# The 24-point stages of batches 2 to 7 fire at the steps of the logits groups, and the first transform of a batch fires during the inverse of the batch before

## The chip, the cores and the metric

The kernel runs on one core of a Trainium2 chip. The metric is the device time of one execution in microseconds (us), taken as the median of several runs. Less is better.

## What is computed

For 8 batches of 3072 x 256 the reference filters in the frequency domain, then runs two token-wise layers. Cut to what matters:

```python
X = np.fft.rfft(x, axis=1)
y = np.fft.irfft(X * (filt_r + 1j * filt_i)[None], n=3072, axis=1)
x = y.reshape(8 * 3072, 256)
h = np.maximum(x @ w_in, 0.0)              # 256 -> 2048
x = h * h @ w_out                          # 2048 -> 256
logits = x @ phi                           # 32 slots
d = softmax(logits, axis=0)                # over all 24576 tokens
slot_out = experts(d.T @ x)                # 8 small experts
out = softmax(logits, axis=1) @ slot_out
```

## The kernel before, in words

The program is written out instruction by instruction, and every engine works through its own list in that order. There are three long phases: a prologue (weights, the whole transform of batch 0), a main loop, and an end with the experts and the output.

**The main loop** runs `pair(P)` for 384 values of P. One pair is 256 of the 2048 hidden features for one chunk of 512 tokens; 8 pairs make a chunk, 48 pairs a batch. A pair has four steps k = 0 to 3, and program time t = 2P + 0.5k counts them, so a batch is 96 units of t. Each step runs `layer` (three matmuls, L380 to L382, in fp32r on the whole array) on PSUM tile p0 in steps 0 and 1 and on p1 in steps 2 and 3. After p0 is full, ScalarE takes relu (L388) and VectorE multiplies (L389, which reads p0 as well, so p0 is free only after it). After p1 is full, ScalarE takes relu (L391) and GpSimd squares (L392). VectorE also transposes both results into hT (L399). In every odd pair, at k = 1, a logits group (`logit`, L408: 4 matmuls, which the profile counts as 8) stands behind the layer.

**The side work** is put into that loop by four streams (`dsp`, `late`, `fft`, `w`). Each entry has a due time; `run_streams` fires entries in order once their time has come, early ones without PSUM tiles ahead of the step's layer, all others behind it. Five PSUM banks are shared by all side work. An entry that needs more banks than are free at that place of the program holds the streams back until a later step.

- `fft` computes the next batch's filtering. `mm_a` (L141 to L143) is the 128-point transform, 12 times a batch: `split_x` (ScalarE L129, GpSimd L130) makes its input, `evac_a` (L151) and `store_a` write it to memory as S. `mm_b` (L187) is the 24-point transform, 8 times a batch, in 16 matmuls (32 in the profile) on 2 banks; `filt` (VectorE L198, two halves of two multiplies each) and `join` (GpSimd L207) apply the filter; `mm_g` (L220) is the inverse 24-point transform on 4 banks, which `evac_g` (ScalarE L229) empties and `store_g` writes to memory as G. Before, batches 2 to 7 have mm_a from t = 5 in steps of 1.5, mm_b at 30 + 6.6 i, and mm_g 4.5 later, all counted from the start of the batch ahead.
- `late` loads G and does the 128-point inverse: `mm_ai` (L320, two halves), `evac_ai` (L330) and `prep` (L343 on ScalarE, L346 on GpSimd), 6 times a batch.
- `dsp` is the softmax over tokens, once a chunk: `gather` (L447) at t = 4 from the chunk's start, `emax` (L452 to L455), `slot_in` (L499, 64 matmuls, 128 in the profile, on 4 banks) at 6.5, directly behind a logits group, and `accum` (VectorE L515) at 8 to 9.5.

The lines that set the order:

```python
    put(T, mm_b, i)                      # T = B0 + i * dB
    put(T + 0.5, filt, i, 0)
    put(T + 1.5, filt, i, 1)
    put(T + n["g"], mm_g, i)
    ...
    if k == 1 and P % 2 and P > 2:
        logit(P - 3)
    run_streams(t)
```

Of the kernel before, what the change touches and what calls it, by code (L numbers as in the profile page):

```python
# [38 lines left out]
def body(tc, x, cA, cAf, fwd, inv, flt, cst, w_in, w_out, phi, w1, w2, out):  # L39
# [10 lines left out]
    G = {}  # L50
# [22 lines left out]
    def put0(t, fn, *a):  # L73
        ev0[round(t, 3)].append((fn, a))
# [23 lines left out]
    def side():  # L98
        if G["nsd"]:
            return G["ps"].tile([128, 512], F32, tag="sd", name="sd", bufs=G["nsd"])  # L100
        k = free.pop(0)
        p = G["ps"].tile([128, 512], F32, tag=f"s{k}", name="sd")
        taken[id(p)] = k, p
        return p

    def done(p):

        if id(p) in taken:
            free.append(taken.pop(id(p))[0])


    def fft_events(b, pl, put, A0, dA, B0, dB, n, st):
        xv = x[b].rearrange("(p n) d -> p n d", n=N2)

        def big():
# [135 lines left out]
        if b == 0:  # L251
# [12 lines left out]
            for i in range(8):  # L264
                T = ST["B0"] + ST["dB"] * i
                put((.7, .75, 15)[i] if i < 3 else T - 6.5, load_c, i)
                put((.8, 9, 15.5)[i] if i < 3 else T - 6.4, load_f, i)
                put(18 + .1 * i if i < 3 else T - 6, load_s, i)
                put(T, mm_b, i)
                for r in range(2):  # L270
                    put(T + 1 + .5 * r, filt, i, r)
                    put(T + 1 + .5 * r, join, i, r)
# [8 lines left out]
        for u in range(12):  # L281
            T = A0 + u * dA
# [2 lines left out]
            put(T + 0.5, evac_a, u)  # L285
            put(T + 2.5, store_a, u)
        for i in range(8):
            T = B0 + i * dB
            put(T - 5.5, load_c, i)
            put(T - 5.5, load_f, i)  # L290
            put(T - 5, load_s, i)
            put(T, mm_b, i)
            put(T + 0.5, filt, i, 0)
            put(T + 1.5, filt, i, 1)
            put(T + 1, join, i, 0)
            put(T + 2, join, i, 1)
            put(T + n["g"], mm_g, i)
            for c in range(4):
                put(T + n["g"] + 0.5 + 0.5 * (c // 2), evac_g, i, c)
            put(T + n["lag"], store_g, i)  # L300

    def out_events(b, st, late):

        def load_g(g):
            t = G["mlp"].tile([128, 4, D], F32, tag="gin", name="gin")
            sync.dma_start(out=t, in_=st["G"][:, 4 * g:4 * g + 4, :])
            st["gi", g] = t

        def warm():

            p = side()
            for _ in range(7):
                pe.matmul(p[:, 0:416], cI, cst_t[:, 0:416], start=True, stop=True)
            done(p)

        def mm_ai(g, k):
            t = st["gi", g]
            p = side()
            for a in range(4):
                pe.matmul(  # L320
                    p[:, 128 * a:128 * a + 128], t[:, a, 128 * k:128 * k + 128], cI,
                    start=True, stop=True,
                )
            st["ai", g, k] = p

        def evac_ai(g, k):
            if k == 0:
                st["xt", g] = G["dsp"].tile([128, 2, CH], F32, tag="xt", name="xt")
            p = st.pop(("ai", g, k))
            act.activation(  # L330
                out=st["xt", g][:, k, :].rearrange("p (q a t) -> p a q t", q=4, a=4),
                in_=p.rearrange("p (a q t) -> p a q t", a=4, q=4), func=ACTF.Copy,
            )
            done(p)

        def prep(g, k):
            xt = st["xt", g]
            if k == 0:
                xo[b * NCB + g] = G["mlp"].tile([128, 2, 2, CH], F32R, tag="xo", name="xo", bufs=2)
            o = xo[b * NCB + g]  # L340
            h = k // 2
            if k % 2 == 0:
                act.activation(out=o[:, 0, h, :], in_=xt[:, h, :], func=ACTF.Copy)  # L343
            else:
                eng = vec if b + g == 0 and h else gps
                eng.tensor_tensor(  # L346
                    out=o[:, 1, h, :], in0=xt[:, h, :], in1=o.bitcast(F32)[:, 0, h, :], op=ALU.subtract
                )

        for g in range(NCB):  # L350
            T = 96 * b + 16 * g - 6
            put = late
            if T < 0:
                def put(t, fn, *a):
                    put0(ST["G0"] + ST["Gd"] * (t + 9), fn, *a)
            put(T - 3, load_g, g)
            if T < 0:
                put(T - 1, warm)
            put(T, mm_ai, g, 0)
            put(T + 0.5, mm_ai, g, 1)  # L360
            put(T + 0.5, evac_ai, g, 0)
            put(T + 1, evac_ai, g, 1)
            for k in range(4):
                put(T + 1.5 + 0.5 * k, prep, g, k)

    xo = {}

# [316 lines left out]
    def stream(nm, o=0):  # L684
        def put(t, fn, *a):
            streams[nm].append((t + o, fn, a))
        return put

    def fire(lst):
        for fn, a in lst:  # L690
            fn(*a)
# [19 lines left out]
    def open_main():  # L711
        first_c.__exit__(None, None, None)
        ps0_c.__exit__(None, None, None)
        G["ps_c"], G["ps"] = pool("ps", 1, PS)
        G["nsd"] = 0
        G["mlp_c"], G["mlp"] = pool("mlp", side="right")
        G["dsp_c"], G["dsp"] = pool("dsp", side="right")
# [36 lines left out]
    with tc.manual_schedule():  # L754
        put, late = stream("fft"), stream("late")
        st = {}
        put0(38, load_const)
        fft_events(0, lambda: first, put0, 0, 0, 0, 0, dict(f=17, u=12, c=4), st)
        out_events(0, st, late)
        def wput(t, *a):  # L760

# [15 lines left out]
        for t in sorted(ev0):  # L777
            if t >= ST["G0"] and not opened:
                opened = True
                open_main()  # L780
            fire(ev0[t])
        for b in range(1, NB):
            st = {}
            fft_events(
                b, lambda: G["fft"], stream("fft", 96 * (b - 1)), *((24, 1.1, 44.2, 4.6) if b == 1 else (5, 1.5, 30, 6.6)), dict(f=6, u=8, c=2, lag=7 if b == 1 else 9.5, g=3.5 if b == 1 else 4.5), st
            )
            out_events(b, st, late)
        for c in range(NCH - 1):
            dispatch_events(c, stream("dsp"))
# [200 lines left out]
        for g in range(NG):  # L990
            b, o = divmod(g, N2 // 4)
# [161 lines left out]
```

## Time and profile before

| | |
|---|---|
| median of 3 runs | 2124.04 us (2123.72 to 2124.53) |
| the profiled execution | 2123.9 us; its span, first to last instruction, 2122.1 us |
| PE (TensorE matmul) busy | 2044.6 us, 96% |
| VectorE (DVE) busy | 1376.1 us, 65% |
| ScalarE (ACT) busy | 887.0 us, 42% |
| GpSimd (POOL) busy | 850.2 us, 40% |
| mean granted TensorE clock | 0.984 of full speed |

A busy PE here is one that has a matmul in flight; starts of matmuls are measured, ends are modelled. So the rows below are read by starts: two neighbouring layer matmuls start 0.23 us apart when nothing hinders them, and what stands between a layer's last start and the next layer's first ones beyond that is the price of what lies between.

### The profile page before, as it was taken

To read this page: it belongs to the slowest core of one execution; us is meant where nothing else is said; L and a number is where in the kernel's file an instruction comes from. 1 tells how busy PE (TensorE), PEld (TensorE's weight loads), DVE (VectorE), ACT (ScalarE), POOL (GpSimd) and SP (SyncE) were. 2 spreads that over 40 slices of the span, in tenths; PEclk is the share of its full clock that TensorE was granted. 3 is DMA by queue.
4 is the path that set the end of the run, shared out by engine and by line. 5 is a ranking of instruction groups with operands and counts; after the bars stand their busy time and mean duration, and the time that the engine had idled before them with its cause. 6 is when DMAs were issued, how large, how long until landed. Compare 5 with 4: busy or idle time off the path is not lost.

```text
span 2122.1 us, 44747 instructions
## 1 busy us (share of the span) xinstructions
PE 2044.6 (96%) x18334; PEld 1287.0 (61%) x18334; DVE 1376.1 (65%) x2516; ACT 887.0 (42%) x1780; POOL 850.2 (40%) x881
## 2 busy tenths in 40 slices
PE   6799999999999999999999999999999999999987
PEld 3366556665666566665566556665566656666556
DVE  3685766566656666576666766667666766666648
ACT  2345434533354344534354334543444334333335
POOL 2425443444353343444344434444345443232324
PEclk7699999999999999999999999999999999999999
DMA  9744342344134332333233332334223433100579
GB/s 286 201 142 135 102 107 74 112 105 120 31 112 116 79 98 65 117 95 110 55 105 105 90 99 67 123 95 110 54 88 102 110 98 94 66 23 12 144 261 384
DMA packets 145037, 238.23 MB, mean 112 GB/s; under 512 B 14785, under 2 KB 97089, under 8 KB 144833
## 3 DMA queue, kind: packets, MB, share of 16 engines
q1 hardware_dynamic: 144688, 235.25, 36.8%
q8 instruction: 144, 2.36, 0.5%
q14 instruction: 61, 0.49, 0.1%
q0 software_dynamic: 144, 0.13, 0.0%
HBM read 154.59 MB, written 80.74 MB: 111 GB/s over the span
## 4 chain that ended last, share of the span: by engine, by line
PE 88%; DVE 6%; DMA 2%; issue 2%; ACT 1%; SPq 0%; POOL 0%; DVEq 0%; ACTq 0%; POOLq 0%
PE p L380 19%; PE p L381 16%; PE p L382 16%; PE sd L499 10%; PE L L408 9%; PE sd L320 4%; PE sd L220 3%; PE sd L187 3%; PE sd L447 2%; DVE u L198 2%; PE sd L141 1%; PE sd L142 1%; PE sd L143 1%; DVE h L389 1%; DVE hT L399 1%
## 5 line engine op out<-in xcount | busy, mean ns | idle before, releaser
L392 POOL TENSOR_TENSOR h<-h 128x512 f32<-128x512 f32 x384 | 399.7, 1041 | 959.6 <-ACT h L391 847.6
L380 PE MATMUL p<-xo,wiH 128*128 128x512 f32 x1536 | 668.7, 435 | 3.9 <-ACT xo L343 1.2
L381 PE MATMUL p<-xo,wiH 128*128 128x512 f32 x1536 | 608.1, 396 | 0.9 <-POOL xo L346 0.9
L382 PE MATMUL p<-xo,wiL 128*128 128x512 f32 x1536 | 607.3, 395 | 0.0
L389 DVE SCALAR_TENSOR_TENSOR h<-p,h 128x512 f32<-128x512 f32 x384 | 264.8, 690 | 448.4 <-ACT h L388 447.3
L399 DVE STREAM_TRANSPOSE hT<-h 128x512 f32<-128x512 f32 x768 | 515.8, 696 | 14.6 <-POOL h L392 3.6
L391 ACT ACTIVATE h<-p 128x512 f32<-128x512 f32 x384 | 229.9, 599 | 540.9 <-PE p L382 539.5
L380 PEld LDWEIGHTS p<-xo,wiH 128*128 128x128 f32 x1536 | 288.8, 188 | 255.6 <-issue 79.3
L388 ACT ACTIVATE h<-p 128x512 f32<-128x512 f32 x384 | 229.6, 598 | 284.3 <-PE p L382 280.9
L382 PEld LDWEIGHTS p<-xo,wiL 128*128 128x128 f32 x1536 | 289.3, 188 | 69.7
L381 PEld LDWEIGHTS p<-xo,wiH 128*128 128x128 f32 x1536 | 290.0, 189 | 58.8 <-issue 9.8
L499 PE MATMUL sd<-hT,eT 32*32 32x512 f32 x6144 | 224.5, 602 | 4.7 <-DVE eT L478 2.9
L207 POOL TENSOR_TENSOR u<-u 128x256 f32<-128x256 f32 x256 | 183.6, 742 | 111.9 <-DVE u L198 111.0
L408 PE MATMUL L<-h,wf 128*32 128x512 f32 x1536 | 205.6, 605 | 0.8 <-POOL h L392 0.8
L198 DVE TENSOR_TENSOR u<-sd,f 128x512 f32<-128x512 f32 x256 | 162.1, 677 | 54.6 <-PE sd L187 54.2
L499 PEld LDWEIGHTS sd<-hT,eT 32*32 32x32 f32 x6144 | 107.5, 103 | 118.3 <-issue 56.5
L515 DVE SCALAR_TENSOR_TENSOR ac<-ac,sc,sd 128x512 f32<-128x512 f32 x188 | 133.8, 733 | 55.0 <-PE sd L499 55.0
L130 POOL TENSOR_TENSOR u<-f,u 128x512 fp32r<-128x512 f32 x84 | 108.0, 1287 | 73.0 <-ACT u L129 72.5
L346 POOL TENSOR_TENSOR xo<-xt,xo 128x512 fp32r<-128x512 f32 x95 | 121.6, 1295 | 6.1 <-ACT xo L343 6.1
L320 PEld LDWEIGHTS sd<-cst_t,gin 128*128 128x128 f32 x768 | 96.6, 191 | 44.4 <-issue 21.8
L229 ACT ACTIVATE f<-sd 128x256 f32<-128x256 f32 x256 | 81.1, 387 | 91.7 <-PE sd L220 91.7
L330 ACT ACTIVATE xt<-sd 128x512 f32<-128x512 f32 x96 | 57.4, 598 | 123.6 <-PE sd L320 123.6
(107 smaller groups left out, 1580.5 us busy)
## 6 DMA issues: line engine op xcount, KB each, us to landing
f<-flt SPq DMA_DIRECT2D x64, 512.0 KB, 4.7
f<-x SPq DMA_DIRECT2D x48, 512.0 KB, 4.2
S<-u SPq DMA_DIRECT2D x96, 256.0 KB, 2.1
f<-S SPq DMA_DIRECT2D x128, 192.0 KB, 5.3
G<-f SPq DMA_DIRECT2D x128, 192.0 KB, 5.2
gin<-G SPq DMA_DIRECT2D x48, 512.0 KB, 6.2
out<-w1t SPq DMA_DIRECT2D x47, 512.0 KB, 5.1
wx<-w SPq DMA_DIRECT2D x34, 256.0 KB, 5.3
```

What stands on the lines that cost most here:

```text
L198: vec.tensor_tensor(out=u, in0=p.rearrange("p (h d) -> p h d", d=D), in1=f[:, 2 * r + k:2 * r + k + 1, :].to_broadcast([128, 2, D]), op=AL ...
L207: gps.tensor_tensor(out=a[:, h, :], in0=a[:, h, :], in1=b[:, 1 - h, :], op=ALU.add if h else ALU.subtract)
L380: pe.matmul(p, wh, x[:, 0, kk, :], start=(kk == 0), stop=False)
L381: pe.matmul(p, wh, x[:, 1, kk, :], start=False, stop=False)
L382: pe.matmul(p, wl, x[:, 0, kk, :], start=False, stop=(kk == 1))
L388: act.activation(out=h, in_=p, func=ACTF.Relu, scale=2.0 ** -16)
L389: vec.scalar_tensor_tensor(out=h, in0=p, scalar=0.0, in1=h, op0=ALU.max, op1=ALU.mult)
L391: act.activation(out=h, in_=p, func=ACTF.Relu, scale=2.0 ** -8)
L392: gps.tensor_tensor(out=h, in0=h, in1=h, op=ALU.mult)
L399: vec.transpose(hT[c][:, 2 * i + k, :], h2[P, k])
L408: pe.matmul(lg[c][32 * n:32 * n + 32, :], wf[:, f, :], h2.pop((P + n // 2, n % 2)), start=(f < 4), stop=(f >= FT - 4), tile_position=(0, 3 ...
L499: pe.matmul(S[r][32 * t:32 * t + 32, :], e[rows, o:o + 32], h[rows, :, o:o + 32], start=(a == 0), stop=(a == 3), tile_position=(32 * r, 32 ...
```

## The change

The functions that compute anything are the same. Three things move.

- For batches 2 to 7, mm_b and mm_g get lists of due times. The list is 4k + 2.5 without every fourth entry, that is, the steps of the logits groups without those that slot_in follows; even entries go to mm_b, odd ones to mm_g. mm_g then follows its mm_b by 4 or 8 units, and store_g follows mm_g by 3.5 (before 5).
- For batches 2 to 7 the first mm_a is due at -22 (before 5), that is, in the last quarter of the batch ahead.
- In the 128-point inverse, of all batches, the second mm_ai moves from T + 0.5 to T + 1, and its evac_ai and all prep by 0.5.

Batch 1 keeps its due times.

```diff
--- before.py
+++ after.py
@@ -109,7 +109,7 @@
             free.append(taken.pop(id(p))[0])
 
 
-    def fft_events(b, pl, put, A0, dA, B0, dB, n, st):
+    def fft_events(b, pl, put, A0, dA, TB, TG, n, st):
         xv = x[b].rearrange("(p n) d -> p n d", n=N2)
 
         def big():
@@ -285,7 +285,7 @@
             put(T + 0.5, evac_a, u)
             put(T + 2.5, store_a, u)
         for i in range(8):
-            T = B0 + i * dB
+            T = TB[i]
             put(T - 5.5, load_c, i)
             put(T - 5.5, load_f, i)
             put(T - 5, load_s, i)
@@ -294,10 +294,11 @@
             put(T + 1.5, filt, i, 1)
             put(T + 1, join, i, 0)
             put(T + 2, join, i, 1)
-            put(T + n["g"], mm_g, i)
+            T = TG[i]
+            put(T, mm_g, i)
             for c in range(4):
-                put(T + n["g"] + 0.5 + 0.5 * (c // 2), evac_g, i, c)
-            put(T + n["lag"], store_g, i)
+                put(T + 0.5 + 0.5 * (c // 2), evac_g, i, c)
+            put(T + 3.5, store_g, i)
 
     def out_events(b, st, late):
 
@@ -357,11 +358,11 @@
             if T < 0:
                 put(T - 1, warm)
             put(T, mm_ai, g, 0)
-            put(T + 0.5, mm_ai, g, 1)
             put(T + 0.5, evac_ai, g, 0)
-            put(T + 1, evac_ai, g, 1)
+            put(T + 1, mm_ai, g, 1)
+            put(T + 1.5, evac_ai, g, 1)
             for k in range(4):
-                put(T + 1.5 + 0.5 * k, prep, g, k)
+                put(T + 2 + 0.5 * k, prep, g, k)
 
     xo = {}
 
@@ -779,11 +780,15 @@
                 opened = True
                 open_main()
             fire(ev0[t])
+
+        grid = [4 * k + 2.5 for k in range(24) if k % 4 != 1]
         for b in range(1, NB):
             st = {}
-            fft_events(
-                b, lambda: G["fft"], stream("fft", 96 * (b - 1)), *((24, 1.1, 44.2, 4.6) if b == 1 else (5, 1.5, 30, 6.6)), dict(f=6, u=8, c=2, lag=7 if b == 1 else 9.5, g=3.5 if b == 1 else 4.5), st
-            )
+            if b == 1:
+                when = (24, 1.1, [44.2 + 4.6 * i for i in range(8)], [47.7 + 4.6 * i for i in range(8)])
+            else:
+                when = (-22, 1.5, grid[0:16:2], grid[1:16:2])
+            fft_events(b, lambda: G["fft"], stream("fft", 96 * (b - 1)), *when, dict(f=6, u=8, c=2), st)
             out_events(b, st, late)
         for c in range(NCH - 1):
             dispatch_events(c, stream("dsp"))
```

**What TensorE issues, at the sixth mm_b of batch 4.** Before, mm_g and mm_b stand together in an even pair (P = 172), with no logits:

```order
L382 MATMUL p<-xo,wiL 128x512
L220 MATMUL sd<-u,iv 64x256 x16
L187 MATMUL sd<-f_10191,fw 32x256 x16
L380 MATMUL p<-xo,wiH 128x512
L381 MATMUL p<-xo,wiH 128x512
L382 MATMUL p<-xo,wiL 128x512
L380 MATMUL p<-xo,wiH 128x512
L381 MATMUL p<-xo,wiH 128x512
L382 MATMUL p<-xo,wiL 128x512
L320 MATMUL sd<-cst_t,gin 128x128 x4
```

Now the same mm_b stands behind the logits of the odd pair that follows (lines below the edit are numbered one higher, so the layer is L381 to L383, logits L409, mm_ai L321):

```order
L321 MATMUL sd<-cst_t,gin 128x128 x4
L381 MATMUL p<-xo,wiH 128x512
L382 MATMUL p<-xo,wiH 128x512
L383 MATMUL p<-xo,wiL 128x512
L409 MATMUL L<-h,wf 32x512 x4
L187 MATMUL sd<-f_10328,fw 32x256 x16
L381 MATMUL p<-xo,wiH 128x512
L382 MATMUL p<-xo,wiH 128x512
L383 MATMUL p<-xo,wiL 128x512
```

The two groups have left the even pair, and mm_g no longer stands in front of mm_b. Over the whole program 42 more mm_g (all 48 of batches 2 to 7 now) and 43 mm_b stand directly behind logits; five further mm_b have one mm_a between. The number of even pairs with no side group between their last p0 matmul and the next pair's first rises from 111 to 154.

**What VectorE issues around a filter.** Before, at the sixth mm_b of batch 4, one transpose stands between the two halves of the filter (L198), and the L389 of the next pair behind them:

```order
L399 STREAM_TRANSPOSE hT<-h 128x512
L198 TENSOR_TENSOR u<-sd,f_10424 128x512 x2
L399 STREAM_TRANSPOSE hT<-h 128x512
L198 TENSOR_TENSOR u<-sd,f_10424 128x512 x2
L389 SCALAR_TENSOR_TENSOR h<-p,h 128x512
L399 STREAM_TRANSPOSE hT<-h 128x512 x2
```

Now, at the seventh mm_b of the same batch, which is one of those at 2.5 units in a chunk (L389 is now L390, L399 is L400, emax L453 to L456):

```order
L390 SCALAR_TENSOR_TENSOR h<-p,h 128x512
L198 TENSOR_TENSOR u<-sd,f_10565 128x512 x2
L400 STREAM_TRANSPOSE hT<-h 128x512 x2
L198 TENSOR_TENSOR u<-sd,f_10565 128x512 x2
L453 TENSOR_REDUCE mn<-sd 128x1
L455 TENSOR_TENSOR mn<-mn 128x1
L456 TENSOR_SCALAR nm<-mn 128x1
L390 SCALAR_TENSOR_TENSOR h<-p,h 128x512
```

Two transposes now stand between the halves, and for the three of eight mm_b that fall at 2.5 the three steps of emax stand between the filter and the L390 that frees p0.

## Rows read from the trace of the kernel before

**Rows 1.** Chain that ended last, by engine (page, part 4).

```profile
PE 88%; DVE 6%; DMA 2%; issue 2%; ACT 1%; SPq 0%; POOL 0%; DVEq 0%; ACTq 0%; POOLq 0%
```

**Rows 2.** Timeline of PE (start us, us, line, operation, out<-in): logits alone.

```profile
1002.81 0.39 PE L382 MATMUL p<-xo,wiL 128*128 128x512 f32 x1
...
1004.46 0.40 PE L381 MATMUL p<-xo,wiH 128*128 128x512 f32 x1
```

**Rows 3.** Timeline of PE: inverse group L220 alone.

```profile
1005.40 0.39 PE L382 MATMUL p<-xo,wiL 128*128 128x512 f32 x1
...
1007.10 0.40 PE L381 MATMUL p<-xo,wiH 128*128 128x512 f32 x1
```

**Rows 4.** Timeline of PE: 24-point group L187 alone.

```profile
1011.28 0.40 PE L382 MATMUL p<-xo,wiL 128*128 128x512 f32 x1
...
1012.97 0.39 PE L381 MATMUL p<-xo,wiH 128*128 128x512 f32 x1
```

**Rows 5.** Timeline of PE: L220 directly behind logits.

```profile
917.90 0.39 PE L382 MATMUL p<-xo,wiL 128*128 128x512 f32 x1
918.22 1.06 PE L408 MATMUL L<-h,wf 128*32 128x512 f32 x8
919.22 1.12 PE L220 MATMUL sd<-u,iv 32*64 32x256 f32 x32
...
920.60 0.40 PE L381 MATMUL p<-xo,wiH 128*128 128x512 f32 x1
```

**Rows 6.** Timeline of PE: L220 and L187 in one step.

```profile
977.93 0.40 PE L382 MATMUL p<-xo,wiL 128*128 128x512 f32 x1
...
979.69 1.10 PE L220 MATMUL sd<-u,iv 32*64 32x256 f32 x26 [0.78 <-DVE ac L515]
981.28 1.37 PE L187 MATMUL sd<-f,fw 48*32 48x256 f32 x32 [0.48 <-ACT f L229]
...
982.92 0.40 PE L381 MATMUL p<-xo,wiH 128*128 128x512 f32 x1
```

**Rows 7.** Timeline of PE: L220 with a wait; slot_in without and with one.

```profile
938.25 1.85 PE L220 MATMUL sd<-u,iv 32*64 32x256 f32 x32
...
970.17 4.47 PE L499 MATMUL sd<-hT,eT 32*32 32x512 f32 x128
...
1014.52 1.05 PE L499 MATMUL sd<-hT,eT 32*32 32x512 f32 x6
1015.87 4.40 PE L499 MATMUL sd<-hT,eT 32*32 32x512 f32 x122 [0.29 <-DVE u L198]
```

**Rows 8.** Timeline of PE: from an even pair to an odd one.

```profile
1010.07 0.39 PE L381 MATMUL p<-xo,wiH 128*128 128x512 f32 x1
1010.30 0.40 PE L382 MATMUL p<-xo,wiL 128*128 128x512 f32 x1
1010.71 0.51 PE L380 MATMUL p<-xo,wiH 128*128 128x512 f32 x1
```

**Rows 9.** Waits, PE: who waited for whom: us in total, times, longest.

```profile
PEld p L380 <- DVE h L389: 52.0, 117, 0.6
```

**Rows 10.** Timeline of DVE, then PE: a filter ahead of L389.

```profile
997.80 1.29 DVE L198 TENSOR_TENSOR u<-sd,f 128x512 f32<-128x512 f32 x2 [0.90 <-PE sd L187]
999.01 0.70 DVE L399 STREAM_TRANSPOSE hT<-h 128x512 f32<-128x512 f32 x1
...
1000.80 0.68 DVE L389 SCALAR_TENSOR_TENSOR h<-p,h 128x512 f32<-128x512 f32 x1
...
1001.54 0.50 PE L380 MATMUL p<-xo,wiH 128*128 128x512 f32 x1
```

**Rows 11.** Timeline of DVE: emax.

```profile
1008.63 0.69 DVE L452 TENSOR_REDUCE mn<-sd 128x1 f32<-128x512 f32 x1 [2.73 <-PE sd L447]
...
1009.55 0.15 DVE L455 TENSOR_SCALAR nm<-mn 128x1 f32<-128x1 f32 x1
```

**Rows 12.** Lines, PE: busy us, mean ns of one, idle before.

```profile
L447 PE MATMUL sd<-lp,cst_t 128*128 128x512 f32 x96 | 49.1, 592 | 0.7 <-ACT lp L442 0.7
```

## The prediction

> **What bounds the kernel now.** I read the chain of waits first, then TensorE's timeline. The chain runs through PE for 88% of the span [rows 1], and PE's list is in order, so almost every gap between PE's starts is time. The gaps are of three kinds, and I price each from starts. Two neighbouring layer matmuls start 0.23 apart [rows 8]; from a layer's last start ahead of a side group to the second layer start behind it would be 0.47 without the group, and the rest is the group's price.
>
> First, the edges of a group. Logits alone cost 1004.46 - 1002.81 - 0.47 = 1.18 [rows 2], an inverse group (mm_g) alone 1.23 [rows 3], a 24-point group (mm_b) alone 1.22 [rows 4]. An inverse group directly behind logits makes 920.60 - 917.90 - 0.47 = 2.23 for both [rows 5]: 0.18 less than the 1.18 + 1.23 apart.
>
> Second, waits for PSUM banks. Where mm_g and mm_b come in one step the pair costs 982.92 - 977.93 - 0.47 = 4.52, with mm_g waiting for accum (L515) and mm_b for mm_g's evacuation (L229) [rows 6]; unhindered they would cost 1.23 + 1.22 = 2.45. A second mm_g takes 1.85 [rows 7] for 1.12 [rows 5]. And slot_in takes 4.47 on most occasions, but from 1014.52 to 1020.27 = 5.75 where mm_b's banks are still held by the filter (L198) [rows 7]. In the timeline each of the three returns once in each of batches 2 to 7.
>
> Third, the step from an even pair to an odd one. p0 is free only when L388 and L389 are through, and if no side group lies between, the next pair's L380 starts 0.41 instead of 0.23 behind the last L382 [rows 8], and its first two steps take 0.57 instead of 0.47 [rows 8, 4]: 0.28 in all. The waits view has PE's weight loads held by L389 117 times [rows 9]. From an odd pair to an even one the logits group gives the slack, so this stall does not occur there.
>
> **The change part by part.** No instruction on TensorE is added or removed; the sum is all about who stands beside whom.
>
> *Edges.* 42 more mm_g stand directly behind logits: 42 x 0.18 = 7.6 saved. For 43 mm_b the trace of before has no case behind logits. The bounds are 0 and the 0.18 of mm_g; I take 0.18, since logits end in the same way for either follower and mm_b alone costs what mm_g alone costs [rows 3, 4]: 7.7. Five mm_b have an mm_a between and save nothing. Together -15.3.
>
> *The bank waits.* mm_g now never falls on accum's steps (8 to 9.5 in a chunk; its places are 2.5, 10.5 and 14.5), it never stands ahead of mm_b in the same step, and no mm_b falls within three units ahead of slot_in. So all three waits should go: 6 x (2.07 + 0.73 + 1.28) = -24.5. At 10.5 mm_g takes four banks of which accum had three or four; it stands behind a whole layer pair and logits, and accum's last read is due a unit earlier, so I add nothing.
>
> *The uncovered step.* mm_b and mm_g used to lie in even pairs about as often as not, and there covered the stall of 0.28. In odd pairs, behind logits, they cover nothing. The order gives 111 uncovered steps before and 154 now: 43 x 0.28 = +12.0.
>
> *The filter ahead of L389.* On VectorE both halves of the filter now stand ahead of the next L389. At such a place before, the chain from 997.80 to 1001.54 made PE wait 0.30, not 0.18 [rows 10]. Now there is one more transpose in it (from 999.01 to 1000.80 are a transpose and a filter half, and a half is 1.21, so 0.58), while PE has half a layer pair more to run, 0.70. So 30 of the 48 are as before or better: 0 (at worst 0.12 each, 3.6). For the 18 at 2.5 emax comes on top: 1008.63 to 1009.70 = 1.07 [rows 11], while PE gets a gather of 49.1 / 48 = 1.02 busy [rows 12], of which its starts feel a little less. Bounds 0 and 0.30 each; I take 0.2: +3.6.
>
> *What I cost at nothing.* The second mm_ai leaves its place behind logits; it uses the whole array like the layer (128*128), so it has no edge to share. If it had, 39 x 0.18 = 7.0 would be lost: kept for the range. The moved transform takes its whole train along: x loads, S stores, splits on ScalarE and GpSimd, and evacuations. On SP's queue each load keeps its lead of 5 units (a unit is some 2.5 us) over its user, and load_g still follows the last store_g by about a unit. On GpSimd the splits now stand beside one filter's joins and on ScalarE beside two inverse groups' evacuations; both engines are under half busy. What covers it is the lead of 2 units that a split has. Without that cover one stretch a batch could cost as much as the waits that go, 4.1.
>
> Sum: 2123.9 (the profiled execution, 0.14 under the median) - 15.3 - 24.5 + 12.0 + 3.6 = 2099.7, say **2100 us**, 1.1% less.
>
> **The rivals.**
>
> *Every change of form drains.* Logits work in 128*32 tiles and mm_b in 48*32 [rows 5, 4]. If the array had to empty between them as it does between layer and mm_b, the 7.7 would not come, and the time is 2107. For it: no row shows this neighbourship. Against it: mm_g's form differs from logits' as well and it saved 0.18. The Trainium skill (TensorEngine Tiling (Array Packing), Key Properties) says that changing the tiling mode, not merely the tile, drains TensorE. By that rule logits followed by mm_b is three changes instead of four, and by it alone the saving would be one drain. No run here yet shows which. Chance 0.10.
>
> *The waits come back in other places.* Five banks serve everything; mm_g takes four, and behind it mm_ai, mm_a or the gather want the fifth and then the ones that ScalarE has just emptied. In the last quarter of each batch mm_a now mixes with both. If half of the 24.5 stays in this form the time is 2112; if all of it, 2124, no change. For it: before, exactly such mixing made the waits. Against it: the new places are 4 units apart or more, and the evacuations are due 0.5 and 1 behind the group. Chance 0.09, of which 0.04 up to no change. That the groups would not follow logits at all is ruled out: the order shows that they do.
>
> *VectorE falls behind and every filter is paid by PE.* VectorE is 65% busy on average, but in a pair of pairs with a filter it has two filter halves, two L389, four transposes and at 2.5 also emax to do, and all in order ahead of the L389 that frees p0. If it enters such a stretch late, as it does when a transpose waits for GpSimd's square behind two joins, PE waits for a whole filter half: 48 x 1.21 = 58, and the time is 2158, **slower**. It turns from gain to loss at 24 / 48 = 0.5 per filter. The Trainium skill (TensorE: Matmul & The Clock Gate, the table at its head) calls VectorE's and GpSimd's queues strictly first in, first out; nothing can pass the filter. The trace agrees so far: L389 starts 3.00 behind the first half, at 1000.80 [rows 10]. Against it: that same place cost PE 0.12 more than usual, not 1.2. Chance 0.04.
>
> **How the numbers follow.** My forecast (waits gone, both kinds of group merged, stall added) has 0.77, and by its own bounds lies from 2093 (no emax term, some mm_a cover more) to 2107 (mm_ai loses its edge). The range goes on to the second rival's half and a little more: **2090 to 2116**. About 0.2% is what a measurement of this kernel can tell from no change, that is 4 us. Faster: 0.77 + 0.10 + 0.05 = 0.92; the same 0.04; slower 0.04.
>
> **What would show it.** In the profile after: L187 starts 1.00 behind logits' start and logits plus L187 cost about 2.23 (if 2.40, the first rival). No L220 waits for L515, and slot_in is about 4.47 everywhere in batches 2 to 7. The weight loads of L380's successor wait for L389 some 150 to 160 times instead of 117, still about 0.28 a piece; behind a mm_b at 2.5 a little more. If these waits grow to over 0.8 a piece the third rival is true. I am wrong if new rows appear in which L320, L141 or L447 wait for L229, or in which L389 waits for L198.

## The result

The changed kernel takes 2100.29 us (median of 5 runs, 2097.76 to 2102.23); the kernel before took 2124.53 in the runs beside it. The ratio is 0.9878, 95% interval 0.9863 to 0.9893: 24 us less, where 24 had been forecast. The range (2090 to 2116) holds it.

### The profile page after: what moved, and what is told of

Its sections match the earlier page's. It is cut to its first block, busy times and chain, and to the rows that moved or that the text cites. A ratio compares the mean times of both kernels' runs of the same rounds, so it can differ in the third digit from the quotient of the medians.

```text
span 2096.9 us, 44709 instructions
## 1 busy us (share of the span) xinstructions
PE 2026.2 (97%) x18334; PEld 1284.7 (61%) x18334; DVE 1370.2 (65%) x2516; ACT 887.4 (42%) x1780; POOL 851.7 (41%) x881
## 4 chain that ended last, share of the span: by engine, by line
PE 87%; DVE 7%; DMA 2%; issue 2%; ACT 1%; POOL 0%; SPq 0%; ACTq 0%; DVEq 0%; POOLq 0%
PE p L381 19%; PE p L382 16%; PE p L383 16%; PE sd L500 10%; PE L L409 9%; PE sd L321 4%; PE sd L220 3%; PE sd L187 3%; DVE u L198 2%; DVE hT L400 1%; PE sd L448 1%; PE sd L141 1%; PE sd L142 1%; PE sd L143 1%; DMA wt<-w_in 1%
## 5 line engine op out<-in xcount | busy, mean ns | idle before, releaser
L381 PE MATMUL p<-xo,wiH 128*128 128x512 f32 x1536 | 672.1, 438 | 7.3 <-DVE h L390 3.5
L383 PE MATMUL p<-xo,wiL 128*128 128x512 f32 x1536 | 607.7, 396 | 0.0
L390 DVE SCALAR_TENSOR_TENSOR h<-p,h 128x512 f32<-128x512 f32 x384 | 265.1, 690 | 438.9 <-ACT h L389 437.5
L400 DVE STREAM_TRANSPOSE hT<-h 128x512 f32<-128x512 f32 x768 | 513.1, 695 | 13.2 <-POOL h L393 2.0
L381 PEld LDWEIGHTS p<-xo,wiH 128*128 128x128 f32 x1536 | 289.1, 188 | 246.3 <-issue 76.2
L389 ACT ACTIVATE h<-p 128x512 f32<-128x512 f32 x384 | 230.1, 599 | 278.8 <-PE p L383 274.0
L383 PEld LDWEIGHTS p<-xo,wiL 128*128 128x128 f32 x1536 | 289.4, 188 | 69.4
L207 POOL TENSOR_TENSOR u<-u 128x256 f32<-128x256 f32 x256 | 184.9, 747 | 171.2 <-DVE u L198 168.9
L500 PE MATMUL sd<-hT,eT 32*32 32x512 f32 x6144 | 217.4, 602 | 4.5 <-DVE eT L479 2.9
L409 PE MATMUL L<-h,wf 128*32 128x512 f32 x1536 | 205.6, 605 | 0.8 <-POOL h L393 0.8
L198 DVE TENSOR_TENSOR u<-sd,f 128x512 f32<-128x512 f32 x256 | 161.8, 675 | 50.8 <-PE sd L187 50.7
L500 PEld LDWEIGHTS sd<-hT,eT 32*32 32x32 f32 x6144 | 103.2, 103 | 115.3 <-issue 63.7
L229 ACT ACTIVATE f<-sd 128x256 f32<-128x256 f32 x256 | 79.8, 387 | 86.7 <-PE sd L220 86.7
L321 PEld LDWEIGHTS sd<-cst_t,gin 128*128 128x128 f32 x768 | 100.4, 191 | 9.7 <-DMA gin<-G 1.4
```

Of the source, the lines that this page charges most:

```text
L198: vec.tensor_tensor(out=u, in0=p.rearrange("p (h d) -> p h d", d=D), in1=f[:, 2 * r + k:2 * r + k + 1, :].to_broadcast([128, 2, D]), op=AL ...
L207: gps.tensor_tensor(out=a[:, h, :], in0=a[:, h, :], in1=b[:, 1 - h, :], op=ALU.add if h else ALU.subtract)
L381: pe.matmul(p, wh, x[:, 0, kk, :], start=(kk == 0), stop=False)
L383: pe.matmul(p, wl, x[:, 0, kk, :], start=False, stop=(kk == 1))
L389: act.activation(out=h, in_=p, func=ACTF.Relu, scale=2.0 ** -16)
L390: vec.scalar_tensor_tensor(out=h, in0=p, scalar=0.0, in1=h, op0=ALU.max, op1=ALU.mult)
```

## The profile after

The profiled execution took 2098.65 us, its span is 2096.9. The page's chain of waits, by engine, answers to [rows 1]:

```profile
PE 87%; DVE 7%; DMA 2%; issue 2%; ACT 1%; POOL 0%; SPq 0%; ACTq 0%; DVEq 0%; POOLq 0%
```

TensorE is still the bound, and VectorE's share of the chain has grown by a point. Where, the timeline shows. First PE around an mm_b at 2.5 units of a chunk of batch 4 (start us, us, line, operation; all lines below the edit are one higher: layer L381 to L383, logits L409, multiply L390):

```profile
834.06 0.39 PE L382 MATMUL p<-xo,wiH 128*128 128x512 f32 x1
834.29 0.40 PE L383 MATMUL p<-xo,wiL 128*128 128x512 f32 x1
834.70 0.50 PE L381 MATMUL p<-xo,wiH 128*128 128x512 f32 x1
...
835.97 0.40 PE L383 MATMUL p<-xo,wiL 128*128 128x512 f32 x1
836.29 1.07 PE L409 MATMUL L<-h,wf 128*32 128x512 f32 x8
837.29 1.09 PE L187 MATMUL sd<-f,fw 48*32 48x256 f32 x32
838.31 0.50 PE L381 MATMUL p<-xo,wiH 128*128 128x512 f32 x1
838.65 0.40 PE L382 MATMUL p<-xo,wiH 128*128 128x512 f32 x1
...
843.24 0.39 PE L383 MATMUL p<-xo,wiL 128*128 128x512 f32 x1
843.83 0.50 PE L381 MATMUL p<-xo,wiH 128*128 128x512 f32 x1 [0.19 <-DVE h L390]
844.16 0.39 PE L382 MATMUL p<-xo,wiH 128*128 128x512 f32 x1
```

Logits and mm_b together cost 838.65 - 835.97 - 0.47 = 2.21; apart they were 1.18 [rows 2] and 1.22 [rows 4]. mm_b starts 837.29 - 836.29 = 1.00 behind the logits, and so did the layer in the kernel before, where nothing stood between (these rows follow the first of [rows 2]):

```profile
1003.13 1.06 PE L408 MATMUL L<-h,wf 128*32 128x512 f32 x8
1004.13 0.50 PE L380 MATMUL p<-xo,wiH 128*128 128x512 f32 x1
```

The ordinary step from an even pair to an odd one is what it was: 834.70 - 834.29 = 0.41 [rows 8]. The step behind a mm_b at 2.5, with emax in the way, is 843.83 - 843.24 = 0.59, so 0.36 over the 0.23 of an unhindered start, and PE itself now shows a wait for L390. VectorE's timeline of the same stretch says why:

```profile
838.48 1.29 DVE L198 TENSOR_TENSOR u<-sd,f 128x512 f32<-128x512 f32 x2 [0.75 <-PE sd L187]
839.68 1.29 DVE L400 STREAM_TRANSPOSE hT<-h 128x512 f32<-128x512 f32 x2
840.90 1.25 DVE L198 TENSOR_TENSOR u<-sd,f 128x512 f32<-128x512 f32 x2
842.07 0.67 DVE L453 TENSOR_REDUCE mn<-sd 128x1 f32<-128x512 f32 x1
842.78 0.20 DVE L455 TENSOR_TENSOR mn<-mn 128x1 f32<-128x1 f32 x1
843.02 0.15 DVE L456 TENSOR_SCALAR nm<-mn 128x1 f32<-128x1 f32 x1
843.09 0.68 DVE L390 SCALAR_TENSOR_TENSOR h<-p,h 128x512 f32<-128x512 f32 x1
```

From 838.48 to 843.77 VectorE has no gap, and the multiply that frees p0 is last. PE's start at 843.83 follows at once. The waits view counts how often L390 holds PE (engine, line, whom it waited for: us in total, times, longest):

```profile
PEld p L381 <- DVE h L390: 73.2, 154, 0.6
...
PE p L381 <- DVE h L390: 3.5, 18, 0.2
```

154 weight loads wait for it, where it was 117 [rows 9], and the 18 steps with emax in which PE waits as well stand in the second row. The bank waits of [rows 6, 7] are gone from batches 2 to 7; what is left of them in the waits view is

```profile
PE sd L187 <- ACT f L229: 4.1, 2, 3.6
...
PE sd L220 <- DVE ac L516: 1.6, 2, 0.8
```

Both waits for accum lie in batch 1, whose due times the change leaves alone; of the two waits for L229 one (0.5) does too, and the long one is in the prologue. In place of the 5.75 and 4.47 of [rows 7], a slot_in of batches 2 to 7 is now usually like this one:

```profile
846.41 4.46 PE L500 MATMUL sd<-hT,eT 32*32 32x512 f32 x128
```

From the first layer matmul's start to the last one's the loop is 25.5 us shorter (98.74 to 2009.80 before, 98.55 to 1984.06 after). All steps without a side group together give back 15.5 us (what their starts have beyond an unhindered 0.467, summed over both timelines, is 32.4 before and 47.9 after), so everything else has brought some 41. Group by group the timelines have 16 for the shared edges, 24.6 for the three waits of [rows 6, 7], 2 for smaller waits of slot_in (six of 0.33) and 1.3 for one wait of batch 1; against these stand some 3 that one slot_in of the changed kernel loses in a pause (last section).

## The experiments

My theory has three parts: a small group directly behind logits saves an edge of 0.18; the three kinds of bank wait came from places close to accum and slot_in; an even pair with no side group behind its p0 matmuls (an uncovered step) stalls for 0.28. The rivals tested: the overlap of batches by itself is the gain; the place of the 128-point inverse is; neighbours do not matter; the stall is not one that other work can fill. Times are medians; the changed kernel's 2100.29 is the mark for the runs from the third on.

**The half step alone.** The kernel before, with mm_ai's second half, its evacuation and prep half a unit later:

```diff
-            put(T + 0.5, mm_ai, g, 1)
             put(T + 0.5, evac_ai, g, 0)
-            put(T + 1, evac_ai, g, 1)
+            put(T + 1, mm_ai, g, 1)
+            put(T + 1.5, evac_ai, g, 1)
             for k in range(4):
-                put(T + 1.5 + 0.5 * k, prep, g, k)
+                put(T + 2 + 0.5 * k, prep, g, k)
```

> The kernel before with one part of the change alone: the second half of the 128-point inverse half a step later. My theory (edges, bank waits, uncovered step): the transposes use the whole array, so leaving the logits neither saves nor costs; 111 uncovered steps as before, bank waits as before: 2124, within 4 us. If they had an edge to lose, 39 x 0.18 = 7: 2131. If the half step were what frees the banks, below 2110.

Measured: 2121.87, ratio 0.9985 (0.9975 to 0.9995). It is a gain of a few us at most. About 1 us of it is seen in the timeline: six mm_g that stood behind logits and mm_ai now stand directly behind logits, and save their edge. Its list of those who waited for L389 (us in total, times) has the weight loads at 117, as before:

```profile
PEld p L380: 51.9, 117
```

mm_ai had no edge to lose, as assumed: behind logits the two cost 2.10, apart 1.19 and 0.89.

**The early transform alone.** The kernel before, with only the first transforms of batches 2 to 7 moved (one line, cut to what changes):

```diff
-    (24, 1.1, 44.2, 4.6) if b == 1 else (5, 1.5, 30, 6.6)
+    (24, 1.1, 44.2, 4.6) if b == 1 else (-22, 1.5, 30, 6.6)
```

> The kernel before with another part alone: the first transform of batches 2 to 7 starts 27 units earlier, the 24-point groups stay. My theory: the overlap by itself brings nothing; the order has 128 uncovered steps for 111, so 17 x 0.28 = 4.8 is lost, and the bank waits stay: 2129 (2125 to 2134). Rival (the overlap of batches is the gain): under 2112.

Measured: 2134.94, ratio 1.0044 (1.0029 to 1.0059): slower, on the side the theory said and by more, 1 us past the expected range. L389 now holds 128 loads, just the number of uncovered steps in the order, and the bank waits are all there. The rest is a wait that I had only named as possible. Rows from its timeline, the weight loads left out:

```profile
1047.46 1.42 POOL L207 TENSOR_TENSOR u<-u 128x256 f32<-128x256 f32 x2
...
1048.88 0.40 PE L382 MATMUL p<-xo,wiL 128*128 128x512 f32 x1
1048.91 0.63 ACT L129 ACTIVATE u<-f 128x512 fp32r<-128x512 f32 x1 [2.49 <-POOL u L207]
1049.45 0.58 ACT L391 ACTIVATE h<-p 128x512 f32<-128x512 f32 x1
...
1050.08 0.50 PE L380 MATMUL p<-xo,wiH 128*128 128x512 f32 x1 [0.81 <-ACT h L391]
...
1050.42 0.39 PE L381 MATMUL p<-xo,wiH 128*128 128x512 f32 x1
```

The split of the next batch's input (L129) needs a buffer that a join (L207) still reads; it stands on ScalarE ahead of the relu that frees p1 (L391), and PE waits 0.81; from start to start it is 1050.42 - 1048.88 - 0.47 = 1.07. This happens in five places, 5.3 in all, which with the 4.8 of the uncovered steps makes up the 10 us. In the changed kernel, with the 24-point groups elsewhere, no such row of PE appears. So the overlap alone costs time and is no gain in itself; it goes with the new places, because the first mm_b, now due at 2.5, comes ahead of the old first mm_a at 5.

**Same kernel, the groups one unit later.** They leave the logits, and the rest of the order stays much as it is:

```diff
-            put(T + 3.5, store_g, i)
+            put(T + 2.5, store_g, i)
...
-        grid = [4 * k + 2.5 for k in range(24) if k % 4 != 1]
+        grid = [4 * k + 3.5 for k in range(24) if k % 4 != 1]
```

> The changed kernel with all 24-point groups of batches 2 to 7 one unit later (end of the odd pair, no longer behind logits; store_g keeps its place). Overlap, uncovered steps (154) and freedom from bank waits stay as they are. My theory: 91 shared edges lost, 91 x 0.18 = +16.4, and the second half of the filter moves behind the multiply that emax delays, -3: 2100 + 13 = 2113. Rival (the groups' neighbours do not matter, only their distance from accum and slot_in): 2100.

Measured: 2109.33, ratio to before 0.9927 (0.9911 to 0.9943): 9 us over the changed kernel, where 13 were expected and the rival said none. Between the two profiles the loop grows by 10.4, and the changed kernel's holds the pause, which this one does not; without it the growth would be 14.5. In the timeline mm_b costs 1.21 and mm_g 1.24 again. The list of those who waited for L390 has no PE row any more, so emax's extra is gone:

```profile
PEld p L381: 71.0, 159
```

The edge is real. The row has 159 waits where the order has 154 uncovered steps; where the other five come from I have not traced.

**Inverse groups back among accum's steps.** The changed kernel with one line edited:

```diff
-    when = (-22, 1.5, grid[0:16:2], grid[1:16:2])
+    when = (-22, 1.5, grid[0:16:2], [t - 1.5 * (t % 16 == 10.5) for t in grid[1:16:2]])
```

> The changed kernel with the 18 inverse groups that stand at 10.5 in a chunk moved to 9.0, among accum's steps. My theory: each waits some 0.75 for accum's third read of its bank, loses its shared edge (0.18) and covers one step (0.28): 18 x 0.65 = +11.7, 2112. In the waits view 18 waits of L220 for L516 come back, some 13 us. Rival (the banks' readers are done in time anyway and the waits of before came from elsewhere): 2098.

Measured: 2119.0, ratio to before 0.997 (0.9957 to 0.9983): 18.7 over the changed kernel, so the rival falls, and the 11.7 was too little. The waits view has the expected row (18 waits more than the changed kernel's 2), and PE's timeline the true size of one:

```profile
PE sd L220 <- DVE ac L516: 15.7, 20, 0.8
```

```profile
939.02 0.39 PE L383 MATMUL p<-xo,wiL 128*128 128x512 f32 x1
939.34 0.65 PE L220 MATMUL sd<-u,iv 32*64 32x256 f32 x6
940.78 1.10 PE L220 MATMUL sd<-u,iv 32*64 32x256 f32 x26 [0.79 <-DVE ac L516]
941.81 0.50 PE L381 MATMUL p<-xo,wiH 128*128 128x512 f32 x1
942.15 0.40 PE L382 MATMUL p<-xo,wiH 128*128 128x512 f32 x1
```

The group costs 942.15 - 939.02 - 0.47 = 2.66 for 1.23 alone: 1.43, of which the bracket shows only 0.79, because six matmuls start on free banks and then run dry. I had taken the 0.75 of the row at 938.25 [rows 7]; the row at 979.69 [rows 6], with six matmuls ahead of the wait, was the one of this kind. With the 1.43 measured here the expectation would have been 18 x (1.43 + 0.18 - 0.28) = 24, more than the 18.7 between the medians; in the two profiles the loop grows by 18.9, and by 23 if the pause in the changed kernel's is left out.

**The gather half a step later.** This fills steps without touching any of the moved groups:

```diff
-        put(q + 2, gather)
-        put(q + 2.5, emax)
-        put(q + 3, expo)
-        put(q + 3.5, turn_e)
-        put(q + 3.5, turn_l)
-        put(q + 4, row_max)
+        put(q + 2.5, gather)
+        put(q + 3, emax)
+        put(q + 3.5, expo)
+        put(q + 4, turn_e)
+        put(q + 4, turn_l)
+        put(q + 4.5, row_max)
```

> The changed kernel with the gather half a step later in every chunk (4.5 instead of 4.0, and emax, expo, turn_e, turn_l and row_max with it), so that it stands between the last p0 matmul of an even pair and the next pair's first. My theory: 39 of 154 uncovered steps are covered, 39 x 0.28 = 10.9, and at 18 of these the longer wait behind emax (0.18 more) goes too, 3.2: 2100 - 14 = 2086, if slot_in does not have to wait for the transposed exponentials (at worst 0.5 in each of 47 chunks, 2110). Rival (the p0 step is not a stall that other work can fill, PE only starts the same work later): 2100.

Measured: 2079.33, ratio to before 0.9786 (0.9773 to 0.98): 21 less than the changed kernel, 14 expected. Those who waited for L390:

```profile
PEld p L381: 52.2, 115
```

154 waits became 115, exactly the 39 steps, and the PE row of 18 is gone. In the profiles the loop is 18.8 shorter: the steps from an even pair to an odd one account for 14.0 of it, as expected, and the pause of one slot_in in the changed kernel's profile, with the lower clock behind it, for 4.1 (last section). The medians differ by 2 us more than the loops; for these I have no proof.

**Nearly every step covered.** On top of that, mm_ai's first half half a unit earlier, and the first transforms from batch 3 on spread over the batch, into steps that were still empty. Cut to its core:

```diff
+        early = [-22 + 1.5 * u for u in range(12)]; spread = [-99.5 + 16 * (u // 2) + 4 * (u % 2) for u in range(12)]
-                when = (-22, 1.5, grid[0:16:2], grid[1:16:2])
+                when = (early if b == 2 else spread, grid[0:16:2], grid[1:16:2])
-            put(T, mm_ai, g, 0)
-            put(T + 0.5, evac_ai, g, 0)
+            put(T - 0.5 * (T > 0), mm_ai, g, 0)
+            put(T + 0.5 - 0.5 * (T > 0), evac_ai, g, 0)
```

> As the run with the gather half a step later; in addition the first half of the 128-point inverse comes half a step earlier (9.5 in a chunk), and from batch 3 on the 12 first-transform groups are spread over the batch at 0.5 and 12.5 of each chunk. 24-point groups stay behind logits. My theory: 28 uncovered steps are left of 154, 126 x 0.28 = 35.3, and emax's 3.2: 2062, if the spread transform brings no new bank wait (each would be some 0.8). Rival (covering has run out, PE is bound by its own matmuls and L390 is late anyway): no better than 2086.

Measured: 2062.15, ratio to before 0.9702 (0.9689 to 0.9716). It beats both kernels, the changed one by 38 us, and meets the 2062 expected. The chain and L390's row in the waits view:

```profile
PE 92%; DVE 3%; issue 2%; DMA 2%; ACT 1%; POOL 0%; SPq 0%; POOLq 0%; ACTq 0%; DVEq 0%
```

```profile
PEld p L381 <- DVE h L390: 12.8, 28, 0.6
```

28 waits are left, as many as the order leaves uncovered (26 of them at the end, where no first transform is left to spread), and VectorE's share of the chain falls from 7% to 3%. Nothing on VectorE became faster (the multiply takes 0.69 as before); PE has other work in the step.

## Why the prediction was right

- *Edges, -15.3.* Right, also the part that no row had shown: logits plus mm_b cost 2.21, so an mm_b saves 0.19. The rival that every change of form drains as it does from the layer, so that mm_b saves nothing, is out: 43 mm_b (and the mm_g, at 2.24 in the timeline) follow logits at 1.00 from start to start, as the layer does. The Trainium skill (TensorEngine Tiling (Array Packing), Key Properties) says that a change of tiling mode drains TensorE. No run here shows a drain by itself; if there is one between logits and mm_b, it is no longer than between logits and the layer, and one change fewer of four is worth the whole 0.18. Moving the groups off the logits again cost 9 us.
- *Bank waits, -24.5.* Right in place and in size. All three kinds are gone from batches 2 to 7, and putting one kind back, mm_g's wait for accum, cost 18.7 us. The other two were not put back; that they went with the move only the two traces show. Smaller waits that the text does not have (2 of slot_in, 1.3 in batch 1) went too.
- *The uncovered step, +12.0, and emax, +3.6.* Right: the steps from an even pair to an odd one have given back 14.9 in the timeline. The ordinary step is unchanged, the 18 with emax are 0.59 instead of 0.41, so 0.18 more each where I took 0.2. That the stall can be filled is shown from the other side by the last two experiments, where the waits for L390 went from 154 to 115 and to 28.
- *At nothing.* The second mm_ai was free to move (run of the half step). The moved train was free in the changed kernel, but not by its own merit: with the 24-point groups in their old places it costs PE 1.07 at five places for want of a buffer. The pause of slot_in was not in the sum at all; its 4 us in the profile and the 3.3 of unforeseen smaller waits nearly cancel, and that the total came out within 1 us is in that much luck.
- *The rivals.* The waits did not come back elsewhere. VectorE did fall behind in the 18 steps with emax, by 0.18 each; the third rival needed 0.5 in each of 48.

## What to carry to other kernels

Where one engine bounds a kernel and its list is fixed, price a piece of side work by its place: here the same 32 matmuls cost 1.22 alone, 1.03 behind another small group, and 1.22 - 0.28 = 0.94 where they fill a wait that the main work has anyway. Count the waits of the main work first and see which of them are empty; the change saved edges of 0.18 and gave up 43 fillings of 0.28, and filling them with other groups brought another 38 us. A bank wait's bracket can show little more than half of its price (0.79 of 1.43): measure from the last start ahead to the second start behind.

## What the runs showed that I had not expected

The order predicts the number of stalls nearly without any time in it. Uncovered steps and waits for the multiply were 111 and 117 in the kernel before and in the run of the half step, 154 and 159 with the groups one unit later, and equal in the others: 154 in the changed kernel, 128, 136, 115 and 28.

In the changed kernel's profile one slot_in pauses, and the waits view names no engine as its cause:

```profile
1357.69 4.42 PE L500 MATMUL sd<-hT,eT 32*32 32x512 f32 x122
1363.70 1.05 PE L500 MATMUL sd<-hT,eT 32*32 32x512 f32 x6 [1.59 <-issue]
...
1366.03 0.63 PE L382 MATMUL p<-xo,wiH 128*128 128x512 f32 x1
1366.46 0.63 PE L383 MATMUL p<-xo,wiL 128*128 128x512 f32 x1
```

The pause costs 2.6 us, and the clock adds to it: from 1366 to 1368 the granted clock is 0.50, the lower of its two levels (1.2 and 2.4 GHz), where it was 1.00 before the pause and is again from 1369 on. In that stretch layer matmuls start 1366.46 - 1366.03 = 0.43 apart instead of 0.23, which costs another 1.5. The last experiment's profile has one such pause with 2.4 on "issue", with the same fall of the clock behind it, and two of 0.8 and 0.9; in the main loop of the other kernels none is of that size. The trace points to instructions that arrive late: PE goes on 2.4 to 3.0 us after a packet of the DMA queue for instructions (q8 in part 3 of the page) has started, in all four pauses. At the two long ones PE had started 514 and 533 matmuls and weight loads between that packet and the one before; but a stretch of 519 in the last experiment passes without a pause. No run varied this, so the cause is not shown.
